# A mixture of experts in pages of 256 tokens: the thirteenth page is cut to 128 rows, and long pages are put ahead of short ones

## The chip, the core and the metric
The kernel runs on one core of a Trainium2 chip. Its metric is the device time of one execution in microseconds. Engines are called PE (TensorE), PEld (its weight loads), DVE (VectorE), ACT (ScalarE), POOL (GpSimd) and SP (SyncE), as the profile has them.

## What is computed
Three layers follow one another. The first is attention with four sink tokens and a window of 128 over 4 batches, 8 heads and 768 positions. The second is a dense layer: `g = h - tanh(h)`, `h = x @ w_in`, then `g @ w_out`. The third, where the change is, sends each of 3072 tokens to one of eight experts:

```python
logits = x @ w_gate + modality_bias[modality_id]
e_idx = np.argmax(logits, axis=1)
gate_w = probs[np.arange(N), e_idx]            # softmax of the logits at e_idx
for e in range(E):
    mask = e_idx == e
    h = np.maximum(x[mask] @ w1[e], 0.0)       # 512 -> 1024
    out[mask] = gate_w[mask, None] * (h @ w2[e])   # 1024 -> 512
```

Counted with the reference on its inputs, two experts get all tokens: 1550 and 1522. In pages of 256 that is seven pages and six. Filled in the order in which tokens come, twelve pages hold 242 tokens or more, and the page opened last, the thirteenth, holds 14.

## The kernel before, in words
Attention and the dense layer run in 12 chunks of 256 tokens. Behind each chunk `r_route` finds the expert of each token, gives each token a slot in a page of 256 slots that belongs to one expert, and writes token number and gate to that slot of a list `xs` in HBM by two scatters on POOL (line 657). `self.rem` holds the free slots of each expert's open page, `self.cur` its next slot, `self.npg` the number of pages so far. Empty slots hold a token number that no write accepts, so that the scatter of the result drops them.

Thirteen pages (`NSTAT`) stand in the main stream, in the order of a table `order` (page and expert of each place). `r_order(False)`, after the eleventh chunk, fills the first three places (`EARLY`) with pages that are already full; `r_order(True)`, after the last, fills the others: rank of each page by a scan (line 684), and then page and expert for each rank by products of 16 x 19 elements and sums over them (lines 692 to 700). SP reads the table into registers (lines 725, 744) and uses them as addresses. What is left, pages from the fourteenth on and the cases that the fast path can't do, stands behind a branch on `self.more` (line 971).

One page is eight blocks of 128 hidden units. `m_list` loads the page's slots of `xs` (line 747), `m_xload` gathers its token rows by two indirect DMAs of 128 rows on POOL (line 762), `m_xT` transposes them on PE (line 773) and splits them into a rounded part and a rest (ACT line 776, DVE line 777). For each block, `m_wload` loads 512 KB of weights, `m_wsplit` splits them on ACT and DVE (lines 738, 739), `m_L1` makes 12 matmuls (line 787; three for each of four 128-slices of the inputs) and the activation (ACT line 790, DVE line 791), `m_L2` makes three matmuls of 512 columns for each of the two halves of 128 tokens (line 804). `m_out` scales the result by the gate (ACT line 812) and scatters 128 rows (POOL line 813), once for each half.

Every operation gets a due time in `m_events` and the like, in units of one block (`t + d` for page start `t` and lead `d`); the events are sorted by it, and a scheduler that simulates the engines then fixes the order in each engine's queue. Each queue is worked in that order. Buffers of one pool go round: the tag `x2` has four, for gathered rows, for results, and for the products of `r_order` (`pv`); sums in PSUM (`macc`) have one buffer for each half. In the table of the order the names `mT2_0`, `macc1_1`, `mx2_0` mean page 2 or 1 and half 0 or 1; `ml2_2` is page 2, block 2.

Of the kernel before, what the change touches and what calls it, by code (L numbers as in the profile page):

```python
# [7 lines left out]
F32 = mybir.dt.float32  # L8
F32R = mybir.dt.float32r
# [31 lines left out]
class Kern:  # L41
# [455 lines left out]
    def r_consts(self):  # L497
# [165 lines left out]
    def r_order(self, last):  # L663
# [7 lines left out]
        bp = lambda ap: ap.unsqueeze(1).to_broadcast([P, NPG, NE])  # L671
        if last:
            v.tensor_scalar(out=sel, in0=self.early, scalar1=-1.0, scalar2=1.0, op0=ALU.mult, op1=ALU.add)
        else:
            end, part, op, big = tl("end", NE), tl("part", NE), tl("op", NPG), cp.tile([P, NPG * NE], F32, tag="pg", name="obig")
            b3 = big.rearrange("p (n e) -> p n e", e=NE)
            v.tensor_add(end, self.cur, self.rem)
            v.tensor_scalar(out=part, in0=self.rem, scalar1=0.0, scalar2=None, op0=ALU.is_gt)
            v.tensor_tensor(out=b3, in0=bn(self.iend), in1=bp(end), op=ALU.is_equal)
            v.tensor_tensor(out=b3, in0=b3, in1=bp(part), op=ALU.mult)  # L680
            v.tensor_reduce(out=op, in_=b3, axis=mybir.AxisListType.X, op=ALU.add)
            v.tensor_scalar(out=sel, in0=self.ipg, scalar1=self.npg, scalar2=None, op0=ALU.is_lt)
            v.tensor_sub(sel, sel, op)
        v.tensor_tensor_scan(out=rk, data0=sel, data1=sel, initial=0.0, op0=ALU.add, op1=ALU.bypass)
# [16 lines left out]
        if last:  # L701
            v.tensor_copy(self.npi, self.npg[:1])

    def r_redo(self, ok):
# [14 lines left out]
        nc.vector.scalar_tensor_tensor(out=t, in0=self.npg, scalar=float(NSTAT), in1=t, op0=ALU.is_le, op1=ALU.mult)  # L719
        self.more = cp.tile([P, 1], I32, name="more")  # L720
# [34 lines left out]
    def m_xload(self, g):  # L755
        nc = self.nc
        pl, idx, src = self.ml[g]
        self.mx[g] = []
        rows = NT - CH if g < EARLY else NT
        for t in range(PG // P):  # L760
# [3 lines left out]
            self.mx[g].append((x, idx[:, t:t + 1], pl[:, t, 0:1]))  # L764

    def m_xT(self, g, t):
        nc = self.nc
        x = self.mx[g][t][0]
        if t == 0:
            self.mxt[g] = self.xtp.tile([P, 2, 4, PG], F32R, tag="xt", name=f"mxt{g}")  # L770
# [8 lines left out]
    def m_L1(self, g, f):  # L779
        nc = self.nc  # L780
        h = self.ps("h", F32, f"mh{g}_{f}")[:, :PG]
# [3 lines left out]
        for k in range(4):  # L785
            for w, xl in ((hi, 0), (hi, 1), (lo, 0)):
                nc.tensor.matmul(h, w[:, k * P:(k + 1) * P], x[:, xl, k], start=(n == 0), stop=(n == 11))  # L787
                n += 1
        gt = self.gp.tile([P, 2, PG], F32R, tag="g", name=f"mg{g}_{f}", bufs=self.o["g"])
# [4 lines left out]
    def m_L2(self, g, f):  # L794
        nc = self.nc
        n8 = FF // P
        if f == 0:
            self.macc[g] = [self.psa.tile([P, DM], F32, tag=f"a{t}", name=f"macc{g}_{t}") for t in range(PG // P)]
# [20 lines left out]
    def m_events(self, add, g, t, t0=-1e9):  # L819
# [9 lines left out]
        at(-x0, self.m_xload, g)  # L829
        for j in range(PG // P):  # L830
            at(-o["mxt"] + 0.5 * j, self.m_xT, g, j)
            at(n8 + o["mlag"] - 0.5, self.m_out, g, j)
        for f in range(n8):
            at(f - o["mwl"], self.m_wload, g, f)
            at(f - o["mws"], self.m_wsplit, g, f)
            at(f, self.m_L1, g, f)
            at(f + o["mlag"], self.m_L2, g, f)
# [198 lines left out]
```

## Time and profile before

| | us |
|---|---|
| median of 3 runs (lowest, highest) | 1171.09 (1169.23, 1175.45) |
| the profiled execution, its own time | 1167.94 |
| its span, first to last instruction | 1166.2 |
| PE busy in the span | 1114.8 |

The page gives shares of the whole span. For a change in one stage it is read by stage: the timeline and the chain of waits from about 1105 us (the last two pages), and from 860 to 885 us (where the last routing, the order and the early pages meet). The profiled execution is 3.15 us below the median.

### The profile page before, as it was taken

What the parts mean: (1) busy time and instruction counts of PE and PEld (TensorE: products, weight loads), DVE (VectorE), ACT (ScalarE), POOL (GpSimd) and SP (SyncE); (2) the same over time, 40 slices, a digit from 0 to 9 for tenths busy, and PEclk for the clock granted to TensorE, in tenths of its full rate; (3) what the DMA queues carried; (4) which work ended last, traced back from release to release, by engine and by line L of the source; (5) the groups of instructions that cost most, each with busy time, mean ns of one, the idle gap of its engine ahead of it and who ended that gap; (6) DMA issues with size and microseconds to landing.
All of it is one profiled execution on the core that took longest, in us unless ns stands there. A gap on an engine that the chain in (4) does not pass through costs nothing.

```text
span 1166.2 us, 22233 instructions
## 1 busy us (share of the span) xinstructions
PE 1114.8 (96%) x7171; PEld 983.8 (84%) x7171; DVE 843.9 (72%) x2229; ACT 697.8 (60%) x1671; POOL 598.1 (51%) x849
## 2 busy tenths in 40 slices
PE   7988889999999999999999999999899999999994
PEld 3456678998999998998999899999788999999994
DVE  3489988787878878797887888756775666666720
ACT  3557556666667666667675766654754556555621
POOL 2367775667676767776676766652322112311210
PEclk9989899999999999999999999999999999999997
DMA  6356322222232222222121312100958776776500
GB/s 200 92 189 227 129 70 49 83 71 73 70 69 81 58 87 68 75 64 87 53 91 55 100 48 87 44 6 28 364 161 251 233 219 210 240 231 220 178 36 4
DMA packets 75117, 137.05 MB, mean 118 GB/s; under 512 B 16240, under 2 KB 51312, under 8 KB 74992
## 3 DMA queue, kind: packets, MB, share of 16 engines
q1 hardware_dynamic: 70064, 122.40, 34.5%
q0 software_dynamic: 4928, 13.14, 3.1%
q8 instruction: 59, 0.97, 0.3%
q14 instruction: 66, 0.54, 0.2%
HBM read 122.86 MB, written 13.17 MB: 117 GB/s over the span
## 4 chain that ended last, share of the span: by engine, by line
PE 76%; DVE 10%; issue 7%; POOL 3%; DMA 1%; ACT 0%; POOLq 0%; DVEq 0%; SPq 0%; ACTq 0%
PE h L176 19%; PE acc L246 18%; PE mh L787 11%; PE macc L804 10%; PE s L315 2%; PE s L312 2%; PE lg L579 2%; PE T L348 2%; PE R L418 2%; PE s L313 1%; DVE K L214 1%; PE T L349 1%; PE R L420 1%; PE R L406 1%; PE xT L572 1%
## 5 line engine op out<-in xcount | busy, mean ns | idle before, releaser
L176 PE MATMUL h<-xt,wi 128*128 128x256 f32 x2304 | 348.3, 289 | 13.3 <-ACT wi L209 5.1
L176 PEld LDWEIGHTS h<-xt,wi 128*128 128x128 f32 x2304 | 311.7, 192 | 32.8 <-ACT wi L209 6.9
L246 PE MATMUL acc<-wo,g 128*128 128x512 f32 x1152 | 315.0, 400 | 4.7 <-ACT g L209 3.7
L246 PEld LDWEIGHTS acc<-wo,g 128*128 128x128 f32 x1152 | 202.5, 190 | 38.4 <-ACT g L209 4.3
L739 DVE TENSOR_TENSOR ml<-mr,mh 128x1024 fp32r<-128x1024 f32 x104 | 128.7, 1242 | 59.7 <-ACT mh L738 57.8
L214 POOL TENSOR_TENSOR g<-gy,g 128x512 fp32r<-128x512 f32 x96 | 130.8, 1362 | 72.5 <-ACT g L209 68.0
L787 PE MATMUL mh<-mxt,mh 128*128 128x256 f32 x832 | 156.1, 283 | 0.7 <-ACT mxt L776 0.7
L804 PE MATMUL macc<-mh,mg 128*128 128x512 f32 x416 | 146.6, 398 | 2.5 <-DVE mg L791 2.5
L787 PEld LDWEIGHTS mh<-mxt,mh 128*128 128x128 f32 x832 | 136.3, 191 | 8.8 <-ACT mxt L776 0.9
L738 ACT CAST mh<-mr 128x1024 fp32r<-128x1024 f32 x104 | 108.9, 1051 | 51.1 <-PE macc L804 31.1
L813 POOL DMA_INDIRECT out_dram<-mo,mi x26 | 27.6, 1061 | 206.5 <-ACT mo L812 202.2
L356 POOL TENSOR_SCALAR_AFFINE_SELECT X<-fl 128x512 fp32r<-128x512 f32 (+1 forms) x192 | 113.2, 612 | 38.7 <-DVE fl L386 23.5
L326 ACT ACTIVATE e<-e,nm 128x160 f32<-128x160 f32 x192 | 81.7, 426 | 80.6 <-DVE nm L324 72.6
L787 PE MATMUL mh<-mxt,ml 128*128 128x256 f32 x416 | 117.6, 284 | 0.0
L191 ACT ACTIVATE u<-u,kt 128x512 f32<-128x512 f32 x96 | 69.4, 723 | 47.0 <-DVE h L190 27.9
L804 PEld LDWEIGHTS macc<-mh,mg 128*128 128x128 f32 x416 | 78.0, 190 | 15.8 <-DVE mg L791 2.9
L214 DVE TENSOR_TENSOR K<-k,K 64x448 fp32r<-64x448 f32 x82 | 85.6, 1044 | 2.7
L214 POOL TENSOR_TENSOR B<-q,A 128x256 fp32r<-128x256 f32 x82 | 70.3, 857 | 33.5 <-ACT A L209 33.3
L324 DVE CUSTOM_DVE_ANT_0 e<-s,mask 128x160 f32<-128x160 f32 x192 | 61.1, 318 | 35.6 <-PE T L349 26.0
L790 ACT ACTIVATE mg<-mh 128x256 fp32r<-128x256 f32 x104 | 40.1, 386 | 73.2 <-PE mh L787 69.8
L804 PE MATMUL macc<-ml,mg 128*128 128x512 f32 x208 | 82.6, 397 | 0.0
L187 ACT ACTIVATE u<-h 128x512 f32<-128x512 f32 x96 | 56.5, 588 | 39.2 <-PE h L176 38.9
(214 smaller groups left out, 2206.4 us busy)
## 6 DMA issues: line engine op xcount, KB each, us to landing
mr<-in_moe_w_dram SPq DMA_DIRECT2D x104, 512.0 KB
k<-in_k_dram SPq DMA_DIRECT2D x82, 224.0 KB
v<-in_v_dram SPq DMA_DIRECT2D x96, 128.0 KB
q<-in_q_dram SPq DMA_DIRECT2D x82, 128.0 KB
rawi<-in_moe_w_in_dram SPq DMA_DIRECT2D x16, 512.0 KB
rawo<-in_moe_w_out_dram SPq DMA_DIRECT2D x16, 512.0 KB
x2d<-x SPq DMA_DIRECT2D x24, 256.0 KB
k<-in_k_dram SPq DMA_DIRECT2D x14, 112.0 KB
```

Of the source, the lines that this page charges most:

```text
L176: nc.tensor.matmul(h, w[:, wl, k * P:(k + 1) * P], x[:, xl, k], start=(n == 0), stop=(n == 11))
L187: nc.scalar.activation(u, h, AF.Square)
L191: nc.scalar.activation(u, u, AF.Relu, bias=self.kt, accum_out=self.over[:, n:n + 1])
L214: (self.nc.vector if eng == "v" else self.nc.gpsimd).tensor_tensor(out=out, in0=a, in1=b, op=ALU.subtract)
L246: nc.tensor.matmul(o, g[:, gl, q:q + P], w[:, wl], start=(f == 0 and n == 0), stop=(f == NF - 1 and n == 2))
L324: nc.vector.tensor_tensor_reduce(out=e, in0=s[:, P:QW], in1=self.mask[min(i, 2)], scale=-0.125, scalar=3.0e38, op0=ALU.add, op1=ALU.min, a ...
L326: nc.scalar.activation(e, e, AF.Exp, bias=nm, scale=-1.0, accum_out=u["sm"][:, t:t + 1])
L356: self.nc.gpsimd.affine_select(out=out, in_=in_, pattern=[[0, n], [s, P]], base=0, channel_multiplier=-s, compare_op=ALU.is_gt if prev els ...
L738: nc.scalar.copy(hi, r)
L739: nc.vector.tensor_sub(lo, r, f32(hi))
L787: nc.tensor.matmul(h, w[:, k * P:(k + 1) * P], x[:, xl, k], start=(n == 0), stop=(n == 11))
L804: nc.tensor.matmul(self.macc[g][t], gt[:, gl, t * P:(t + 1) * P], w[:, DM:], start=(f == 0 and n == 0), stop=(f == n8 - 1 and n == 2))
```

## The change
Of the thirteenth place only the first half (128 rows) stays in the main stream: gather, transposes, matmuls, activation and result take a list of halves `ts`, which is `(0,)` there and `(0, 1)` elsewhere. Its second half moves behind the branch. `r_order(True)` now ranks pages with more than 128 tokens ahead of the others, so that the page at the thirteenth place has more than 128 only if ten such pages stand outside the early three; that is `self.half`, which also makes `self.more` true. So that it can tell, it uses `rem`, `cur` and `npg` as the last chunk leaves them, where the rank before came from `early` alone and only the experts (`pexp`) waited for the last chunk. Line numbers shift: 738, 739, 747, 762, 787, 791, 804 and 813 become 753, 754, 762, 777, 803, 807, 820 and 829; 657 becomes 658; 692 to 700 become 705 to 713.

```diff
--- before.py
+++ after.py
@@ r_consts
+        self.half = cp.tile([P, 1], F32, name="half")
-        self.npi = cp.tile([1, 1], I32, name="npi")
+        self.npi = cp.tile([1, 2], I32, name="npi")
@@ r_order(last)
+        end, part, op, big = tl("end", NE), tl("part", NE), tl("op", NPG), cp.tile([P, NPG * NE], F32, tag="pg", name=nm + "big")
+        b3 = big.rearrange("p (n e) -> p n e", e=NE)
+        v.tensor_add(end, self.cur, self.rem)
+        v.tensor_scalar(out=part, in0=self.rem, scalar1=float(PG // 2) if last else 0.0, scalar2=None,
+                        op0=ALU.is_ge if last else ALU.is_gt)
+        v.tensor_tensor(out=b3, in0=bn(self.iend), in1=bp(end), op=ALU.is_equal)
+        v.tensor_tensor(out=b3, in0=b3, in1=bp(part), op=ALU.mult)
+        v.tensor_reduce(out=op, in_=b3, axis=mybir.AxisListType.X, op=ALU.add)
+        v.tensor_scalar(out=sel, in0=self.ipg, scalar1=self.npg, scalar2=None, op0=ALU.is_lt)
+        v.tensor_sub(sel, sel, op)
         if last:
-            v.tensor_scalar(out=sel, in0=self.early, scalar1=-1.0, scalar2=1.0, op0=ALU.mult, op1=ALU.add)
+            all_, rs = tl("all", NPG), tl("rs", NPG)
+            v.tensor_scalar(out=all_, in0=self.early, scalar1=-1.0, scalar2=1.0, op0=ALU.mult, op1=ALU.add)
+            v.tensor_mul(sel, sel, all_)
+            v.tensor_tensor_scan(out=rk, data0=sel, data1=sel, initial=0.0, op0=ALU.add, op1=ALU.bypass)
+            v.tensor_sub(op, all_, sel)
+            v.tensor_tensor_scan(out=rs, data0=op, data1=op, initial=rk[:, NPG - 1:], op0=ALU.add, op1=ALU.bypass)
+            v.tensor_scalar(out=self.half, in0=rk[:, NPG - 1:], scalar1=float(NSTAT - EARLY), scalar2=None, op0=ALU.is_ge)
+            v.tensor_mul(rk, rk, sel)
+            v.tensor_mul(rs, rs, op)
+            v.tensor_add(rk, rk, rs)
+            sel = all_
         else:
...
+            v.tensor_tensor_scan(out=rk, data0=sel, data1=sel, initial=0.0, op0=ALU.add, op1=ALU.bypass)
         v.tensor_sub(rk, rk, sel)
...
-            v.tensor_copy(self.npi, self.npg[:1])
+            v.tensor_copy(self.npi[:, :1], self.npg[:1])
+            v.tensor_copy(self.npi[:, 1:], self.half[:1])
@@ r_redo
         nc.vector.scalar_tensor_tensor(out=t, in0=self.npg, scalar=float(NSTAT), in1=t, op0=ALU.is_le, op1=ALU.mult)
+        nc.vector.scalar_tensor_tensor(out=t, in0=self.half, scalar=0.0, in1=t, op0=ALU.is_equal, op1=ALU.mult)
@@ m_xload, m_xT, m_L1, m_L2, m_events: a list ts of row blocks
-        for t in range(PG // P):
+        for t in ts:
...
-    def m_L1(self, g, f):
+    def m_L1(self, g, f, ts):
+        c0, w = ts[0] * P, len(ts) * P
-        h = self.ps("h", F32, f"mh{g}_{f}")[:, :PG]
+        h = self.ps("h", F32, f"mh{g}_{f}")[:, :w]
...
-                nc.tensor.matmul(h, w[:, k * P:(k + 1) * P], x[:, xl, k], start=(n == 0), stop=(n == 11))
+                nc.tensor.matmul(h, wt[:, k * P:(k + 1) * P], x[:, xl, k, c0:c0 + w], start=(n == 0), stop=(n == 11))
...
-        for t in range(PG // P):
+        for i, t in enumerate(ts):
...
-                nc.tensor.matmul(self.macc[g][t], gt[:, gl, t * P:(t + 1) * P], w[:, DM:],
+                nc.tensor.matmul(self.macc[g][t], gt[:, gl, i * P:(i + 1) * P], w[:, DM:],
@@ run_chunks
             for g in range(NSTAT):
                 self.m_events(add, g, 16.0 * nch + self.o["mt0"] + FF // P * g,
-                              first if g < EARLY else t2 + self.o["trr"] + .35)
+                              first if g < EARLY else t2 + self.o["trr"] + .35,
+                              (0, 1) if g < NSTAT - 1 else (0,))
@@ more_pages
+            half = nc.values_load(self.npi[0:1, 1:2], min_val=0, max_val=1)
             np_ = nc.values_load(self.npi[0:1, 0:1], min_val=0, max_val=NPG)
+            def page(g, ts=(0, 1)):
+                ev = []
+                self.m_events(lambda t, fn, *a: ev.append((t, len(ev), fn, a)), g, 0.0, ts=ts)
+                self.emit(ev)
+            with tc.If(half == 1):
+                page(NSTAT - 1, (1,))
```

POOL, behind the last routing: the two scatters to `xs` stand behind the gathers of page 2 before:

```order
L762 DMA mx2_0_12228<-x2d_64,ms2_11561 128x512
L762 DMA mx2_1_12230<-x2d_64,ms2_11561 128x512
L657 DMA xs_63<-pl_336,sl11_12141 4864x2 x2
L813 DMA out_0_dram<-mo0_0_12270,mi0_11527 3072x512
L813 DMA out_0_dram<-mo0_1_12275,mi0_11527 3072x512
```

and now:

```order
L658 DMA xs_63<-pl_336,sl11_12142 4864x2 x2
L777 DMA mx2_0_12251<-x2d_64,ms2_11562 128x512
L777 DMA mx2_1_12253<-x2d_64,ms2_11562 128x512
L829 DMA out_0_dram<-mo0_0_12293,mi0_11528 3072x512
L829 DMA out_0_dram<-mo0_1_12298,mi0_11528 3072x512
```

The gathers of page 2 have moved behind the two scatters; the rest keeps its order.

VectorE, from the last slots of the routing on (`sl`). Before, the order was written by then, and the queue went on with weights (`ml`) and activations (`mg`):

```order
L649 CAST sl11_12141<-slf11_12140 128x2
L777 TENSOR_TENSOR mxt1_12177<-mT1_1_12219,mxt1_12177 128x4x128
L721 TENSOR_SCALAR more_12201<-ovt_12195 128x1
L739 TENSOR_TENSOR ml2_2_12464<-mr2_2_12258,mh2_2_12463 128x1024
L791 SCALAR_TENSOR_TENSOR mg1_0_12255<-mh1_0_12242,mg1_0_12255 128x256
L739 TENSOR_TENSOR ml2_3_12518<-mr2_3_12296,mh2_3_12517 128x1024
L791 SCALAR_TENSOR_TENSOR mg1_1_12293<-mh1_1_12280,mg1_1_12293 128x256
L739 TENSOR_TENSOR ml2_4_12546<-mr2_4_12326,mh2_4_12545 128x1024
L751 SCALAR_TENSOR_TENSOR ms3_12505<-mpl3_12501 128x2
L739 TENSOR_TENSOR ml2_5_12586<-mr2_5_12363,mh2_5_12585 128x1024
L791 SCALAR_TENSOR_TENSOR mg1_2_12323<-mh1_2_12310,mg1_2_12323 128x256
```

Now the order's operations stand there. These are the last twelve of them, behind fifteen on rows of 1 to 152 elements that come after `sl`:

```order
L736 TENSOR_SCALAR more_12224<-ovt_12217 128x1
L807 SCALAR_TENSOR_TENSOR mg1_0_12278<-mh1_0_12265,mg1_0_12278 128x256
L694 TENSOR_TENSOR olrk_12163<-olrk_12163,olrs_12176 128x19
L698 TENSOR_TENSOR olrk_12163<-olrk_12163,olall_12175 128x19
L705 TENSOR_TENSOR olpv_12187<-ipg_332,olrk_12163 128x304
L807 SCALAR_TENSOR_TENSOR mg1_1_12316<-mh1_1_12303,mg1_1_12316 128x256
L706 TENSOR_TENSOR olpv_12187<-olpv_12187,olall_12175 128x304
L709 TENSOR_TENSOR olpv_12187<-olpv_12187,ipg_332 128x304
L710 TENSOR_REDUCE olres_12190<-olpv_12187 128x16
L709 TENSOR_TENSOR olpv_12187<-olpv_12187,pexp_342 128x304
L713 CAST order_344<-olres_12190 1x16
L710 TENSOR_REDUCE olres_12190<-olpv_12187 128x16
```

All sixteen-rank products have moved behind the routing, with two activations (`mg1_0`, `mg1_1`) between; the weights `ml2_2` come behind them.

PE, at the first sums of page 1. Before:

```order
L773 MATMUL mT2_1_12483<-ident_69,mx2_1_12230 128x128 x4
L804 MATMUL macc1_0_12298<-mh1_0_12039,mg1_0_12255 128x512
L804 MATMUL macc1_0_12298<-ml1_0_12040,mg1_0_12255 128x512
L804 MATMUL macc1_1_12299<-mh1_0_12039,mg1_0_12255 128x512
L804 MATMUL macc1_1_12299<-ml1_0_12040,mg1_0_12255 128x512
```

and now:

```order
L803 MATMUL mh1_3_12361<-mxt1_12199,ml1_3_12262 128x256
L788 MATMUL mT2_0_12479<-ident_69,mx2_0_12251 128x128 x4
L788 MATMUL mT2_1_12506<-ident_69,mx2_1_12253 128x128 x4
L820 MATMUL macc1_1_12322<-mh1_0_12040,mg1_0_12278 128x512
L820 MATMUL macc1_1_12322<-ml1_0_12041,mg1_0_12278 128x512
```

Both transposes of page 2 have moved behind the fourth block of page 1, and the sums of the second half (`macc1_1`) of blocks 0 and 1 behind those.

## Rows read from the trace of the kernel before

**Rows 1.** The page, part 1: busy time, share of the span and instructions of each engine.
```profile
PE 1114.8 (96%) x7171; PEld 983.8 (84%) x7171; DVE 843.9 (72%) x2229; ACT 697.8 (60%) x1671; POOL 598.1 (51%) x849
```
**Rows 2.** The chain that ended last, from 1060 us: start us, us, what.
```profile
1105.15 0.44 PE mT L773 x4
...
1114.89 1.39 PE macc L804 x6
1116.27 1.43 PE mh L787 x12
```
**Rows 3.** Busy time in the stretch of the thirteenth page: engines, PEclk, DMA share, GB/s.
```profile
1128.30:1151.50 23.20, 23.14 (x147) 20.68 (x145) 3.54 (x9) 4.58 (x11) 1.95 (x2) 1.00 0.06 22
```
**Rows 4.** Timeline of weight loads from 399.8 us: start us, us, what.
```profile
399.89 0.19 PEld L416 LDWEIGHTS R<-X,V 128*128 128x128 f32 x1
400.00 0.30 PEld L418 LDWEIGHTS R<-X,V 128*128 128x128 f32 x2
400.23 0.30 PEld L420 LDWEIGHTS R<-X,V 128*128 128x128 f32 x2
400.45 0.42 PEld L176 LDWEIGHTS h<-xt,wi 128*128 128x128 f32 x3
```
**Rows 5.** The chain, from 835 us: gate logits, eight columns each.
```profile
848.62 0.79 PE lg L579 x8
```
**Rows 6.** POOL at the end, then DMA queues from 1148 us on.
```profile
1152.22 0.97 POOL L813 DMA_INDIRECT out_dram<-mo,mi  x1 [20.16 <-ACT mo L812]
1153.49 0.97 POOL L813 DMA_INDIRECT out_dram<-mo,mi  x1 [0.30 <-issue]
...
q0 software_dynamic: 160, 0.03, 0.9%
```
**Rows 7.** Timeline of VectorE: first order, at 806 us; second order, at 865 us.
```profile
806.78 0.16 DVE L677 TENSOR_TENSOR oeend<-cur,rem 128x8 f32<-128x8 f32 x1
...
806.98 0.32 DVE L679 TENSOR_TENSOR obig<-iend,oeend 128x152 f32<-128x152 f32 x1
807.33 0.32 DVE L680 TENSOR_TENSOR obig<-obig,oepart 128x152 f32<-128x152 f32 x1
...
808.69 0.18 DVE L687 SCALAR_TENSOR_TENSOR early<-oerk,oesel 128x19 f32<-128x19 f32 x1
...
865.10 0.47 DVE L696 TENSOR_TENSOR olpv<-olpv,pexp 128x304 bf16<-128x304 bf16 x1
...
865.70 0.46 DVE L697 TENSOR_REDUCE olres<-olpv 128x16 f32<-128x304 bf16 x1
...
866.60 0.15 DVE L649 CAST sl<-slf 128x2 int32<-128x2 f32 x1
```
**Rows 8.** Matmuls and VectorE at page 1, the chain there, and a window after it.
```profile
866.65 0.51 PE L787 MATMUL mh<-mxt,mh 128*128 128x256 f32 x2 [0.68 <-ACT mxt L776]
...
879.76 0.73 PE L804 MATMUL macc<-mh,mg 128*128 128x512 f32 x2 [2.45 <-DVE mg L791]
...
878.01 0.16 DVE L751 SCALAR_TENSOR_TENSOR ms<-mpl 128x2 int32<-128x2 f32 x1 [3.83 <-DMA mpl<-xs]
...
868.35 6.98 DMA xs<-pl,sl
...
880.00:884.00 4.00, 4.00 (x18) 3.62 (x18) 2.74 (x4) 2.10 (x4) 2.24 (x2) 0.60 0.90 296
```
**Rows 9.** DMA issues of the whole span: median us from issue to landing.
```profile
mx<-x2d,ms POOLq DMA_INDIRECT x26, 6.7
...
xs<-pl,sl POOLq DMA_INDIRECT x24, 3.9
```
**Rows 10.** Timeline of matmuls inside that window.
```profile
881.84 0.63 PE L787 MATMUL mh<-mxt,mh 128*128 128x256 f32 x2
...
882.48 0.63 PE L804 MATMUL macc<-mh,mg 128*128 128x512 f32 x1
882.91 0.63 PE L804 MATMUL macc<-ml,mg 128*128 128x512 f32 x1
```

More of the change, by code (lines that the diff above doesn't have):

```diff
@@ L671, in r_order @@
         bp = lambda ap: ap.unsqueeze(1).to_broadcast([P, NPG, NE])
-        if last:
-            v.tensor_scalar(out=sel, in0=self.early, scalar1=-1.0, scalar2=1.0, op0=ALU.mult, op1=ALU.add)
-        else:
[L675 to L683, printed above, removed]
@@ L785, in m_L1 @@
         for k in range(4):
-            for w, xl in ((hi, 0), (hi, 1), (lo, 0)):
-                nc.tensor.matmul(h, w[:, k * P:(k + 1) * P], x[:, xl, k], start=(n == 0), stop=(n == 11))
+            for wt, xl in ((hi, 0), (hi, 1), (lo, 0)):
+                nc.tensor.matmul(h, wt[:, k * P:(k + 1) * P], x[:, xl, k, c0:c0 + w], start=(n == 0), stop=(n == 11))
                 n += 1
-        gt = self.gp.tile([P, 2, PG], F32R, tag="g", name=f"mg{g}_{f}", bufs=self.o["g"])
+        gt = self.gp.tile([P, 2, PG], F32R, tag="g", name=f"mg{g}_{f}", bufs=self.o["g"])[:, :, :w]
         nc.scalar.activation(gt[:, 0], h, AF.Relu)
@@ L792, in m_L1, with m_L2 @@
         self.mg[g, f] = gt
-    def m_L2(self, g, f):
+    def m_L2(self, g, f, ts):
         nc = self.nc
@@ L797, in m_L2 @@
         if f == 0:
-            self.macc[g] = [self.psa.tile([P, DM], F32, tag=f"a{t}", name=f"macc{g}_{t}") for t in range(PG // P)]
+            self.macc[g] = {t: self.psa.tile([P, DM], F32, tag=f"a{t}", name=f"macc{g}_{t}") for t in ts}
         gt = self.mg.pop((g, f))
         hi, lo = self.mw.pop((g, f))
-        for t in range(PG // P):
+        for i, t in enumerate(ts):
             n = 0
             for gl, w in ((0, hi), (0, lo), (1, hi)):
-                nc.tensor.matmul(self.macc[g][t], gt[:, gl, t * P:(t + 1) * P], w[:, DM:],
+                nc.tensor.matmul(self.macc[g][t], gt[:, gl, i * P:(i + 1) * P], w[:, DM:],
                                  start=(f == 0 and n == 0), stop=(f == n8 - 1 and n == 2))
@@ L817, in m_out, with m_events @@
         self.sc = i.ins
-    def m_events(self, add, g, t, t0=-1e9):
+    def m_events(self, add, g, t, t0=-1e9, ts=(0, 1)):
         n8 = FF // P
@@ L828, in m_events @@
             at(-x0 - .01, self.m_list, g)
-        at(-x0, self.m_xload, g)
-        for j in range(PG // P):
-            at(-o["mxt"] + 0.5 * j, self.m_xT, g, j)
+        at(-x0, self.m_xload, g, ts)
+        for j in ts:
+            at(-o["mxt"] + 0.5 * j, self.m_xT, g, j, ts)
             at(n8 + o["mlag"] - 0.5, self.m_out, g, j)
@@ L835, in m_events @@
             at(f - o["mws"], self.m_wsplit, g, f)
-            at(f, self.m_L1, g, f)
-            at(f + o["mlag"], self.m_L2, g, f)
+            at(f, self.m_L1, g, f, ts)
+            at(f + o["mlag"], self.m_L2, g, f, ts)
     def emit(self, ev):
@@ L944, in rest @@
                 with tc.If(np_ > g):
-                    ev = []
-                    self.m_events(lambda t, fn, *a: ev.append((t, len(ev), fn, a)), g, 0.0)
-                    self.emit(ev)
+                    page(g)
                     rest(g + 1)
```

11 lines of the change are left out of this document (5 added, 6 removed).

## The prediction
> **What bounds the kernel now.** The page comes first: PE is busy for 96% of the span and no other engine over 84% [rows 1], so only what PE does, or waits for, can move the end. The chain that ended last comes second. In the last pages it runs on PE alone, in a fixed pattern: 1.43 us for the 12 matmuls of a block's first layer, 1.39 us for the six of its second, and 0.44 us for each half's four transposes [rows 2]. That is 0.119 us for a matmul of 256 columns and 0.232 us for one of 512. The window of the thirteenth page shows PE busy for 23.14 of 23.20 us at a granted clock of 1.00, with DVE, ACT and POOL nearly idle and DMA at 0.06 [rows 3]: weights are in place, and a cut of PE's work shows at the end. Behind PE stand two scatters on POOL, 1.27 us apart [rows 6]. The third view is the timeline at page 1, where the last routing meets the early pages. PE waited 2.45 us there for an activation, because DVE stood for 3.83 us at the list of page 3, which waited for the scatters to `xs` [rows 8]. The clock then fell: 0.60 in the window from 880 to 884 us [rows 8].
>
> **The half page.** The table gives the thirteenth place to the page with 14 tokens, in both kernels: the scatters at the end moved 0.03 MB, some 15 rows of 2 KB, where one half of full rows is 0.26 MB [rows 6]. Its second half is all padding. Nine pages with over 128 tokens stand outside the early three (twelve less three), less than ten, so `half` is 0 and the branch isn't taken. What goes:
> - Second layer: 24 of 48 matmuls of 512 columns, 24 x 0.232 = **5.57 us**.
> - First layer: the 96 matmuls stay, with 128 columns in place of 256. Their weight loads stay whole, and the trace has their price: loads beside matmuls of 128 columns start 0.11 us apart (399.89, 400.00; the two from 400.23 to 400.45) [rows 4], and transposes of 128 columns take 0.44 / 4 = 0.11 [rows 2]. Even matmuls of eight columns take 0.79 / 8 = 0.099 [rows 5]. So half the columns are nearly as dear: 96 x (0.119 - 0.11) = **0.86 us**. Ends: nothing (0.119 each), and 1.9 us (0.099 each). I take 0.11, from the rows with the same columns.
> - Transposes of the second half: **0.44 us** [rows 2].
> - The last scatter: the end moves up by the distance of the two, **1.27 us** [rows 6]; what follows it is the same.
>
> The Trainium skill, TensorE: Matmul & The Clock Gate, section Back-to-back issue gap, speaks of a stream of weight loads and matmuls that runs at about 81 ns a matmul with 128 columns. By it the first layer would give back 96 x 0.038 = 3.6 us in place of 0.86. The rows above, on this kernel's four-byte weights, show 110 ns, and the measurement decides.
>
> Activations and splits of the half page are shorter, and their engines idle [rows 3]. Its weights still come whole, under page 11. Together this is 8.14 us, all on the path.
>
> **The order, which must now wait for the last chunk.** Before, 16-rank products ran ahead of the routing's end, and only a product, a sum and a cast came late. Now all of it comes behind `sl`, which itself is done some 0.85 us earlier than 866.60, since two long operations ahead of it are gone [rows 7]. The first order did the like of eight of the new operations in 808.69 - 806.78 = 1.9 us, 0.35 apart where they have 152 elements [rows 7]. Seven small ones more are about 1.2 us, six long ones 6 x 0.52 = 3.1 (0.47 and a gap) [rows 7], four small ones 0.6, and the three operations between (a split, two activations) 1.5: 8.3 us, so the table is ready near 874 us, not 866. Who waits:
> - SP, which reads the table for page 3's list and weights. Page 3 starts two pages of over 23 us [rows 3] after page 1, which began at 866.65 [rows 8]. Eight microseconds are covered. If the cover were gone, PE would wait for the rest.
> - ACT: the result of page 0's second half goes to the buffer that holds the products. ACT stops there until the last sum, and activations and splits queue behind it. The order has PE's sums `macc1_1`, which need that result taken out, three blocks' work later.
> - DVE's splits of page 2 come later, but page 2 is a page away.
> - POOL: the gathers of page 2 now issue behind the scatters: those at about 866.1 and 867.4, the gathers at 868.7 and 870.0. With 6.7 us to landing [rows 9] the rows are there at 875.4 and 876.7.
>
> PE from 866.65 on: four blocks of first layer are 5.7 us, three sums each of two blocks 1.4, the wait for the split 0.6: it comes to page 2's transposes at 874.3. There it waits 1.1 us, and 0.85 more for the second half. This stands in the place of the old 2.45 us, for page 3's list now lands when DVE has weights to split. I take a gain of 0.4 us. Ends: both the old wait and the low clock behind it go ((1 - 0.60) x 4.0 = 1.6 us more [rows 8]), with no new wait, a gain of 4.1; or the new wait adds to what DVE does late, a loss of 3.
>
> **Sum.** 8.14 + 0.4 = 8.5 us. The profiled execution took 1167.94, so 1159.4; it lies 3.15 below the median of the runs, so the forecast for a median is **1162.5 us**.
>
> **Rivals.**
> - *More comes back.* The wait at page 1 goes with its low clock (12.2 us in all, 1158.8), or matmuls of 128 columns cost half of those with 256 (96 x 0.06 = 5.7 in place of 0.86, so 13.3 us in all, 1157.7). For: the list is no longer ahead of the weights on DVE; the chain's x4 and x8 groups are too short to be a steady stream [rows 2, 5]. Against: weight loads 0.11 apart [rows 4]. Chance 0.15.
> - *A new wait at the order.* If DVE's late chain takes six microseconds more than worked out, ACT is released near 881 us, `macc1_1` with it, and PE waits some 4 us over the old wait: -8.14 + 4 and up to 1.6 for the clock, 1167 to 1168.6. For: every one of some thirty operations waits for the one before, in one queue with activations that PE needs. Against: prices from the same operations [rows 7], and no other work in the queue. Chance 0.12; it counts as no change.
> - *Slower: PE falls to its lower level in the half page.* With 128 columns the array works for less of the time. At 1.2 GHz three first-layer matmuls took 882.48 - 881.84 = 0.64 us, and one of 512 columns 0.43 [rows 10]; the half page would be 96 x 0.213 + 24 x 0.43 = 30.8 us in place of 16.1, which is 14.6 more and 6 us slower than before: 1177. It decides from the point where 8.5 / 14.6 = 58% of the page runs at that level. For: the level fell soon after a wait of 2.45 us [rows 8]. Against: PE has a next matmul ready all through this page [rows 3], and weight loads go on without a gap. Chance 0.04.
> - *It doesn't do what it says.* If `half` were 1, the second half would run behind the branch with its own weight loads, 16 us of PE's work and more: over 1175. The 0.03 MB [rows 6] speak against it. Chance 0.01.
>
> **Numbers.** The forecast has the other 0.68, with 1159.5 to 1165.5 by the ends of its terms. About 0.5%, 5.9 us, is what a measurement of this kernel can tell from no change. Forecast and first rival are faster, 0.83; the new wait is no change, 0.12; the last two are slower, 0.05. The range, 1157 to 1168, takes in the first rival and most of the second.
>
> **What would show it.** First layer of the thirteenth page: 96 matmuls of 128 columns, 0.11 us apart; 600 second-layer matmuls in place of 624; one scatter at the end. PE's span for that page is 16 to 16.5 us against 23.2. At page 1, PE waits for the transposes of page 2, two microseconds in all, and the table is cast near 874 us. The prediction is wrong if spacing is 0.06 or 0.12, if the clock there is below 1.00, or if PE waits more than 5 us between 866 and 885.

## The result, and the profile after

The changed kernel took 1159.42 us (median of 4 runs, 1158.06 to 1160.81) against 1170.38 for the kernel before in the same session (4 runs, 1169.23 to 1175.45): a ratio of 0.9898, 95% interval 0.9866 to 0.9930, so 11 us less. Two later timings, of six runs each, gave 0.9907 (0.9874 to 0.9941) and 0.9900 (0.9863 to 0.9937). The forecast was 1162.5, in a range of 1157 to 1168. The profiled execution took 1158.06 with a span of 1156.3, 9.9 us under the span before.

The page's part 1, which answers to [rows 1]:

```profile
PE 1109.8 (96%) x7143; PEld 978.2 (85%) x7143; DVE 845.4 (73%) x2244; ACT 696.1 (60%) x1669; POOL 586.4 (51%) x847
```

PE has 28 matmuls less: 24 of the second layer and 4 transposes; 96 of the first layer are only shorter. Its busy time falls by 5.0 us and the span by 9.9: the rest is time in which PE waited, or what stands behind its last matmul.

Where the span went is read from the starts of the stages in the timeline (the first first-layer matmul of a chunk or a page); the three columns on the right are the changed kernel's three profiles.

| stage, us | before | after | again | third |
|---|---|---|---|---|
| first chunk to the second | 99.98 | 98.21 | 98.24 | 105.89 |
| second chunk to the twelfth | 626.42 | 626.67 | 626.90 | 626.84 |
| twelfth chunk to the last gate logits | 74.42 | 75.18 | 75.67 | 74.48 |
| last gate logits to page 1 | 11.89 | 11.90 | 11.90 | 11.89 |
| page 1 to page 2 | 27.38 | 25.32 | 24.46 | 24.43 |
| page 2 to page 3 | 23.43 | 23.43 | 23.43 | 23.43 |
| page 3 to page 4 | 23.42 | 23.84 | 23.42 | 23.42 |
| page 4 to page 11 | 163.99 | 163.99 | 164.00 | 163.99 |
| page 11 to the last sum | 46.57 | 40.25 | 40.24 | 40.25 |
| last sum to the end | 14.75 | 13.54 | 13.72 | 13.86 |

From page 1 on, where the change is, the first profile is 9.2 us shorter than before, the other two 10.3 and 10.2; the rest of the 9.9 us lies ahead of page 1 (1.8 less in the first chunk, 1.0 more in the two stretches behind it). The 0.4 us more from page 3 to page 4 in the first profile stand in neither of the others.

**The half page.** 6.3 us come back by the last sum and 0.9 to 1.2 behind it. (The last stage varies by itself: 14.37 to 15.25 us in the four profiles with two scatters at the end, 13.34 to 14.25 in the ten with one.) The window from its first matmul to its last, with columns as in [rows 3]:

```profile
1124.95:1142.80 17.85, 17.85 (x127) 16.16 (x125) 2.79 (x10) 3.48 (x10) 1.94 (x2) 1.00 0.07 29
```

PE waits for nothing, at a clock of 1.00. One block in PE's timeline (start us, us, what; the rows of short matmuls overlap, some 0.28 us long and 0.11 apart, so the starts are read):

```profile
1133.78 0.33 PE L803 MATMUL mh<-mxt,mh 128*128 128x128 f32 x2
1133.95 0.28 PE L803 MATMUL mh<-mxt,ml 128*128 128x128 f32 x1
1134.07 0.39 PE L803 MATMUL mh<-mxt,mh 128*128 128x128 f32 x2
1134.29 0.28 PE L803 MATMUL mh<-mxt,ml 128*128 128x128 f32 x1
...
1135.07 0.44 PE L820 MATMUL macc<-mh,mg 128*128 128x512 f32 x1
...
1135.82 0.33 PE L803 MATMUL mh<-mxt,mh 128*128 128x128 f32 x2
```

From 1133.95 to 1134.07 is one matmul, from 1134.07 to 1134.29 two: 0.11 us each. The twelve take 1.29 us and the three of the second layer 0.75, where it was 1.43 and 1.39 [rows 2]: 2.04 a block in place of 2.82. Behind the last sum only one scatter is left; it answers to the two of [rows 6]:

```profile
1143.80 0.97 POOL L829 DMA_INDIRECT out_dram<-mo,mi  x1 [12.95 <-ACT mo L828]
```

**The order.** On VectorE the slots of the last chunk (`sl`), the end of the table, and page 3's list:

```profile
865.28 0.17 DVE L650 CAST sl<-slf 128x2 int32<-128x2 f32 x1
...
872.92 0.16 DVE L713 CAST order<-olres 1x16 int32<-1x16 f32 x1
...
882.27 0.17 DVE L764 CAST mi<-mpl 128x2 int32<-128x2 f32 x1
```

The list landed at 881.58 us, and VectorE, which came to it from splitting weights, didn't wait for it. On ScalarE the result of page 0's second half, which waits for the buffer of the products:

```profile
872.92 0.69 ACT L828 ACTIVATE mo<-macc,mpl 128x512 f32<-128x512 f32 x1 [2.33 <-DVE olres L710]
```

On POOL the scatters to `xs` and the gathers of page 2, one after the other:

```profile
865.74 1.03 POOL L658 DMA_INDIRECT xs<-pl,sl  x1 [26.17 <-DVE olpart L677]
867.07 1.00 POOL L658 DMA_INDIRECT xs<-pl,sl  x1 [0.30 <-issue]
868.38 0.98 POOL L777 DMA_INDIRECT mx<-x2d,ms  x1 [0.30 <-issue]
869.67 1.13 POOL L777 DMA_INDIRECT mx<-x2d,ms  x1 [0.31 <-PE mh L803]
```

And PE, its waits in page 1 and the transposes of page 3:

```profile
866.70 0.38 PE L803 MATMUL mh<-mxt,mh 128*128 128x256 f32 x1 [0.22 <-DVE mxt L792]
...
875.00 1.38 PE L788 MATMUL mT<-ident,mx 128*128 128x128 f32 x8 [1.14 <-DMA mx<-x2d,ms]
...
891.41 0.60 PE L788 MATMUL mT<-ident,mx 128*128 128x128 f32 x4
```

The wait of 2.45 us behind page 3's list is gone, with one of 1.14 us for page 2's rows in its place, and the granted clock, which was 0.60 in the window behind the old wait [rows 8], stays at 1.00:

```profile
876.00:878.00 2.00, 2.00 (x12) 1.50 (x11) 0.41 (x1) 0.82 (x2) 0.00 (x0) 1.00 0.86 281
880.00:882.00 2.00, 2.00 (x13) 1.74 (x13) 2.00 (x3) 1.93 (x4) 0.00 (x0) 1.00 1.03 393
```

Page 1 to page 2 is 2.1 us shorter than before, and 2.9 in the two later profiles, where the wait for page 2's rows is 0 and 0.27 us.

### The profile page after: what moved, and what is told of

The parts are those of the page before. It is cut to its first block, busy times and chain, and to the rows that moved or that the text cites. A ratio compares the mean times of both kernels' runs of the same rounds, so it can differ in the third digit from the quotient of the medians.

```text
span 1156.3 us, 22180 instructions
## 1 busy us (share of the span) xinstructions
PE 1109.8 (96%) x7143; PEld 978.2 (85%) x7143; DVE 845.4 (73%) x2244; ACT 696.1 (60%) x1669; POOL 586.4 (51%) x847
## 5 line engine op out<-in xcount | busy, mean ns | idle before, releaser
L803 PE MATMUL mh<-mxt,mh 128*128 128x256 f32 (+1 forms) x832 | 154.4, 282 | 1.0 <-ACT mxt L791 0.7
L820 PE MATMUL macc<-mh,mg 128*128 128x512 f32 x400 | 141.6, 399 | 0.2
L803 PE MATMUL mh<-mxt,ml 128*128 128x256 f32 (+1 forms) x416 | 117.0, 282 | 0.0
L820 PEld LDWEIGHTS macc<-mh,mg 128*128 128x128 f32 x400 | 74.4, 189 | 13.3 <-DVE mg L807 1.0
L806 ACT ACTIVATE mg<-mh 128x256 fp32r<-128x256 f32 (+1 forms) x104 | 39.2, 377 | 75.1 <-PE mh L803 70.6
L803 PEld LDWEIGHTS mh<-mxt,ml 128*128 128x128 f32 x416 | 79.3, 191 | 0.0
```

The lines of the kernel that those rows point to most:

```text
L803: nc.tensor.matmul(h, wt[:, k * P:(k + 1) * P], x[:, xl, k, c0:c0 + w], start=(n == 0), stop=(n == 11))
L820: nc.tensor.matmul(self.macc[g][t], gt[:, gl, i * P:(i + 1) * P], w[:, DM:], start=(f == 0 and n == 0), stop=(f == n8 - 1 and n == 2))
```

## The experiments

Theory: the half page and the order are separate gains, some 7.5 us at the end and some 2 to 3 at page 1, the second because VectorE no longer stands at page 3's list ahead of work that PE needs. Rivals: that wait and the low clock behind it vary by themselves; the long order costs something that the half page hides; short matmuls are priced by columns. Ratios are to the kernel before, timed beside.

**half_old_rank: the half page alone**

```diff
-        end, part, op, big = tl("end", NE), tl("part", NE), tl("op", NPG), cp.tile([P, NPG * NE], F32, tag="pg", name=nm + "big")
...
+        if last:
+            v.tensor_scalar(out=sel, in0=self.early, scalar1=-1.0, scalar2=1.0, op0=ALU.mult, op1=ALU.add)
...
-            with tc.If(half == 1):
-                page(NSTAT - 1, (1,))
```

> The half page alone: the rank is the one of before (from `early` alone), so the scatters, the list of page 3 and all else up to the last page stand in the queues as before. It leaves out the guard: a thirteenth page with over 128 tokens would lose its second half. Theory (the two gains are separate, and the order stage gave its 2.1 us by moving page 3's list out of VectorE's way): the half page gives 7.5 us here too (matmuls of 128 columns 0.112 us apart, 2.04 us a block in place of 2.82, one scatter 1.2 us earlier), while at page 1 the wait of 2.45 us behind page 3's list and the granted clock near 0.6 after it are back: page 1 to page 2 start 27.4 us, span 1166.2 - 7.5 = 1158.7. Rival (the wait at page 1 and the low clock vary from execution to execution, and the changed kernel only drew a better one): page 1 to page 2 near 25.3 or less here as well, span 1156.5. Rival (the half page is worth more when nothing else changes, 128-column matmuls hidden behind loads): block under 1.9 us.

Ratio 0.9909 (0.9883 to 0.9935). From page 11 on it is the changed kernel (40.25 us to the last sum, 13.35 behind it). At page 1 the old wait is back, longer. VectorE's timeline there:

```profile
881.30 0.16 DVE L752 SCALAR_TENSOR_TENSOR ms<-mpl 128x2 int32<-128x2 f32 x1 [5.79 <-DMA mpl<-xs]
```

PE's, where it waits for the activation behind that list:

```profile
883.05 0.73 PE L806 MATMUL macc<-mh,mg 128*128 128x512 f32 x2 [3.35 <-DVE mg L793]
```

The windows from then on, with the granted clock third from the end:

```profile
882.00:884.00 2.00, 0.95 (x5) 0.86 (x6) 1.29 (x4) 1.30 (x2) 1.45 (x2) 0.93 0.81 266
884.00:886.00 2.00, 2.00 (x11) 2.00 (x11) 1.34 (x2) 0.99 (x2) 1.84 (x1) 0.50 0.90 309
```

Page 1 to page 2 took 28.27 us. The theory holds: 7.7 us belong to the half page alone (46.57 + 14.75 less 40.25 + 13.35), and the wait and low clock come with the old order of VectorE's queue.

**rank_full_page: the new order alone**

```diff
-                              (0, 1) if g < NSTAT - 1 else (0,))
+                              (0, 1))
...
-            with tc.If(half == 1):
-                page(NSTAT - 1, (1,))
```

> The new order alone: long pages ranked ahead, all of the order behind the last routing, but the thirteenth page is computed whole, as before. Theory: page 1 to page 2 start 25.3 us as in the changed kernel (a wait of 1.1 us for the gathers of page 2, clock 1.00), so 2.1 us come back there and some 0.4 are lost at page 3's list: span 1164.0 to 1164.5, some 2 us under before. Rival (the longer order costs time, and the gain of the changed kernel is all the half page's): span 1166 or more. Last page as before: 2.82 us a block, two scatters 1.27 us apart.

Ratio 0.9969 (0.9949 to 0.9989): the new order by itself is faster. Page 1 to page 2 took 24.56 us, 0.7 less than expected, for the wait for page 2's rows was 0.4 us and not 1.1. PE's waits in that stretch are 0.7 and 0.2 us for page 1's splits and this one (what waited, for what, us in total, times, longest):

```profile
PE mT L788 <- DMA mx<-x2d,ms: 0.4, 1, 0.4
```

The last page is as before (23.15 us, 14.43 behind). The span came out at 1166.6 and not 1164, since the first chunk took 1.3 us more than in the profile of the kernel before (101.2 us) and the stretch from the twelfth chunk to the last logits 1.8 more. The first chunk has nothing of the change and took 96.2 to 105.9 us in the fourteen profiles, which is why only stages and medians are compared here.

**before_late_list and before_pool_list: the kernel before, page 3's list later in VectorE's queue, or on GpSimd**

The first makes the list of page 3, and with it the gathers of its rows, due four blocks later; the second has a page's list (from page 3 on) made into addresses by GpSimd:

```diff
         x0 = o["mxe"] if g == 1 else o["mxl"]
+        x0 -= 4 if g == 3 else 0
```
```diff
-        nc.vector.tensor_copy(idx, pl[:, :, 1])
...
-        nc.vector.scalar_tensor_tensor(out=src, in0=pl[:, :, 1], scalar=float(NT), in1=pl[:, :, 1], op0=ALU.is_lt, op1=ALU.mult)
+        if g >= EARLY:
...
+            nc.gpsimd.tensor_copy(idx, pl[:, :, 1])
+            nc.gpsimd.tensor_scalar(out=lt, in0=pl[:, :, 1], scalar1=float(NT), scalar2=None, op0=ALU.is_lt)
+            nc.gpsimd.tensor_mul(lt, lt, pl[:, :, 1])
+            nc.gpsimd.tensor_copy(src, lt)
...
```

> The kernel before with one edit: the list of page 3 is due four blocks later, so that on VectorE its operation stands behind the split of the last block of page 2's weights. Theory (the old wait came from the place of that operation in VectorE's queue, ahead of weights and activations that PE needs): the wait of 2.45 us and the low clock after it both go, page 1 to page 2 start 23.5 to 24 us in place of 27.4, span 1162.3 to 1162.8. Rival (the low clock comes from something else in this stretch, the load of 0.9 of DMA for one): the wait goes and the clock still falls, page 1 to page 2 near 25, span 1163.8. Rival (the wait only moves to the next thing that is late): 27 us, span 1166.

> The kernel before with the same move of the list's operations to GpSimd and nothing else: PE's and ScalarE's order is that of before, VectorE's differs by those operations alone. Theory (the wait of 2.45 us and the low clock behind it came from VectorE's stand at the list, and from nothing else): page 1 to page 2 start 23.4 us in place of 27.4, no low clock in that stretch, 4.0 us less from page 1 on and all else as before; so of the changed kernel's gain the part at page 1 (2.1 us there) is to be had, and more of it, without a new order. Rival (GpSimd, which stands at the list now, issues the results and rows behind it late): PE waits elsewhere in pages 1 to 3, and less than 2 us come back.

Ratios 0.9960 (0.9937 to 0.9984) and 0.9963 (0.9938 to 0.9988); page 1 to page 2 took 23.39 and 23.15 us, the pace of the other pages. In the first, VectorE stands at the list as long as before, but behind six splits of weights in page 1 and not three:

```profile
881.27 0.17 DVE L749 CAST mi<-mpl 128x2 int32<-128x2 f32 x1 [3.90 <-DMA mpl<-xs]
```

PE waits for nothing behind it. In the second, GpSimd's waits from 866 to 920 us hold the list now:

```profile
POOL mlt L753 <- DMA mpl<-xs: 10.4, 2, 7.8
```

and all that is left of PE's, from 862 to 916 us, is

```profile
PE mh L794 <- ACT mxt L783: 0.7, 1, 0.7
```

So the cause was the place of the list's operations in VectorE's queue, ahead of work that PE needed, and not the stand of 3.8 or 3.9 us as such; 4.0 and 4.2 us were to be had there without any new order.

**own_buffer: the products of the order in a buffer of their own**

```diff
-        pv = self.x2p.tile([P, DM], F32, tag="x2", name=nm + "pv").bitcast(BF16)
-        pick, val = pv[:, :n * NPG], pv[:, DM:DM + n * NPG]
+        pick = cp.tile([P, (NPG - EARLY) * NPG], BF16, tag="opk", name=nm + "pk")[:, :n * NPG]
+        val = cp.tile([P, NPG * NE], F32, tag="pg", name=nm + "pv").bitcast(BF16)[:, :n * NPG]
```

> The changed kernel with one edit: the products of the order lie in a buffer of 608 bytes of their own and in the routing's scratch, no longer in one of the four buffers for rows. The gathers of page 2 then stand ahead of the scatters again, their transposes at page 1's first block, and ScalarE takes out page 0's second half without waiting for the order. Theory (the products' buffer was what put the gathers behind the scatters and held ScalarE 2.33 us): the wait of 1.14 us for the gathers goes, page 1 to page 2 start 23.5 to 24.2 us, span 1154.9 to 1155.5, clock 1.00. Rival (the scatters, now 2.6 us later, make page 3's list late and VectorE waits for it): a wait for the list of some us on VectorE comes back, PE waits over 1 us at page 1 again, span 1156.5 or more.

Ratio 0.9906 (0.9877 to 0.9934), no more than the changed kernel. The wait for page 2's rows is gone and ScalarE takes out page 0 at 863.92 and 865.07 us, but VectorE's timeline has the wait for the list again:

```profile
881.36 0.17 DVE L764 CAST mi<-mpl 128x2 int32<-128x2 f32 x1 [2.34 <-DMA mpl<-xs]
```

and PE's one for ScalarE at the end of the page:

```profile
888.37 0.50 PE L820 MATMUL macc<-mh,mg 128*128 128x512 f32 x1 [0.57 <-ACT mg L806]
```

Page 1 to page 4 took 71.47 us (before 74.23; the changed kernel 72.59, 71.31, 71.28), and that without four of page 2's transposes, 0.44 us, which here (and in the two runs that follow) stand ahead of page 1. The buffer did what was said of it, and what was next in line took the gain.

**own_buffer_late_list and own_buffer_pool_list: both cures together**

Own_buffer with the one or the other of the two edits to the list above.

> Both cures on the changed kernel: the order's products in a buffer of their own, and the list of page 3 due four blocks later. Theory: VectorE no longer waits 2.34 us for that list in page 1, so the 0.57 us that PE waited at its end and the 0.44 us in page 2 go too: page 1 to page 2 start 23.4 to 23.6 us, page 2 to page 3 23.4 us, 1.2 us under own_buffer and 1.9 under the changed kernel from page 1 on; span 1153.5 if the first chunk is as there. Rival (the list, four blocks later, makes the rows of page 3 late): a wait for transposes in page 2, and no gain over own_buffer.

> The changed kernel with the order's products in a buffer of their own, as in own_buffer, and the two operations on the list of a page (its token numbers made integers, from page 3 on) on GpSimd as four small ones, ahead of the gathers that use them; nobody else reads them. SyncE issues the list where it did in own_buffer. Theory (what was left in own_buffer is VectorE's stand of 2.34 us at the list, with weights and activations behind it, and moving the list's due time moved its issue and the stand with it): VectorE waits for no list any more, page 1 to page 2 start 23.3 to 23.6 us, page 2 to page 3 23.43, 1.0 to 1.2 us under own_buffer from page 1 on. Rival (the wait comes back as late rows, since GpSimd stands at the list too): PE waits for transposes of page 3 in page 2.

Both miss. Ratios 0.9925 (0.9900 to 0.9950) and 0.9932 (0.9906 to 0.9958); page 1 to page 2 is 23.10 and 23.12 us, and page 2 to page 3 then 25.64 and 27.64. In the first, SyncE issues the list at 885.47 us, ten later than in own_buffer, and the stand in VectorE's timeline moves with it:

```profile
890.89 0.17 DVE L764 CAST mi<-mpl 128x2 int32<-128x2 f32 x1 [2.17 <-DMA mpl<-xs]
```

PE waits behind it, in page 2:

```profile
894.59 0.73 PE L820 MATMUL macc<-mh,mg 128*128 128x512 f32 x2 [1.91 <-DVE mg L807]
```

In the second, the list is issued as in own_buffer (875.07 us), lands at 880.89, GpSimd's gathers start at 884.08 and 885.44, the rows land at 890.44 and 892.03, and PE has stood at their transposes since 888.06, as its timeline shows:

```profile
890.58 0.63 PE L795 MATMUL mT<-ident,mx 128*128 128x128 f32 x4 [2.52 <-DMA mx<-x2d,ms]
```

Of those 2.52 us, 1.7 come from GpSimd. Two of its four operations on the list stand in its timeline as

```profile
881.63 1.05 POOL L769 TENSOR_TENSOR mlt<-mlt,mpl 128x2 f32<-128x2 f32 x1
882.74 1.06 POOL L770 CAST ms<-mlt 128x2 int32<-128x2 f32 x1
```

where the same two took 0.20 and 0.18 us in before_pool_list; here VectorE was splitting weights at the time (`ml`, 881.40 to 883.76 us).

The windows behind PE's wait:

```profile
890.00:892.00 2.00, 1.42 (x8) 1.31 (x9) 0.00 (x0) 0.52 (x1) 0.00 (x0) 0.83 0.84 338
892.00:894.00 2.00, 2.00 (x11) 2.00 (x10) 0.00 (x0) 0.74 (x2) 1.25 (x2) 0.50 0.08 23
```

PE's queue has the transposes of page 3 at the start of page 2, not of page 3. In the changed kernel's first profile page 3's first rows landed at 890.11 us and were transposed at 891.41: the long order had 1.3 us to spare there. In its other two profiles it was 0.35 and 0.34 us (landed 890.96, transposed 891.31; 897.30, 897.64), against 10.6 with the old order in half_old_rank.

**long_order: 6 us more on the chain**

```diff
+            for _ in range(6 if last else 0):
+                v.tensor_reduce(out=res[:, i * n:(i + 1) * n], in_=v3, axis=mybir.AxisListType.X, op=ALU.add)
```

> The changed kernel with twelve more sums over 304 elements in the order (the two sums of the products are each taken seven times), 6 us more on VectorE's chain: the condition of the rival with the new wait. Theory (ScalarE stands at page 0's second result until the last sum, and PE's sums of page 1's second half wait for ScalarE): the table is cast near 879 us in place of 873, ScalarE goes on then, PE waits 3.5 to 4.5 us more than the 1.4 of the changed kernel at page 1, the granted clock falls behind that wait, and page 1 to page 2 start is 29 to 31 us: 4 to 5.5 us slower. Rival (there is slack in the chain): under 27 us. Rival (6 us cost 6 us and more, since weights queue behind): over 31.5 us.

Ratio 0.9977 (0.9954 to 1.0001). The size is right and the place wrong: page 1 to page 2 took 25.13 us, page 2 to page 3 28.55. On VectorE the table is written at

```profile
885.04 0.17 DVE L715 CAST order<-olres 1x16 int32<-1x16 f32 x1
```

which is 15.8 us after page 1's start, where the changed kernel has 7.0: nine more, not six, since activations of page 1 stand inside the chain now. ScalarE's hold cost PE 0.67 and 0.34 us. The rest came by way of the list (table, list, rows), in page 2 of PE's timeline:

```profile
895.69 0.73 PE L822 MATMUL macc<-mh,mg 128*128 128x512 f32 x2 [1.06 <-DVE mg L809]
901.72 0.63 PE L790 MATMUL mT<-ident,mx 128*128 128x128 f32 x4 [2.09 <-DMA mx<-x2d,ms]
```

with the clock behind it, in the windows:

```profile
902.00:904.00 2.00, 2.00 (x10) 1.62 (x8) 0.62 (x1) 0.34 (x1) 0.00 (x0) 0.68 1.00 401
904.00:906.00 2.00, 2.00 (x11) 1.90 (x10) 1.22 (x1) 0.70 (x1) 0.00 (x0) 0.50 1.03 402
```

**half_64: what a short matmul costs**

```diff
-        c0, w = ts[0] * P, len(ts) * P
+        c0, w = ts[0] * P, len(ts) * P if ts != (0,) else P // 2
...
```

> The changed kernel with the first layer of the thirteenth page cut to 64 columns, and its sums, result and scatter to 64 rows; rows 64 to 127 of that page are left out (here it has 14 tokens). Theory (weight loads set the price of short matmuls): first-layer matmuls stay 0.10 to 0.112 us apart, second-layer matmuls 0.232, a block 1.9 to 2.05 us; the page gives 0 to 1.1 us more. Rival (columns set the price): 0.06 us apart, 1.4 us a block, 5 us more.

Ratio 0.9925 (0.9895 to 0.9956). A block takes 1.97 us in place of 2.04, the page 0.40 less. One block's first layer in PE's timeline:

```profile
1132.19 0.30 PE L803 MATMUL mh<-mxt,mh 128*128 128x64 f32 x2
1132.33 0.28 PE L803 MATMUL mh<-mxt,ml 128*128 128x64 f32 x1
1132.44 0.39 PE L803 MATMUL mh<-mxt,mh 128*128 128x64 f32 x2
1132.67 0.28 PE L803 MATMUL mh<-mxt,ml 128*128 128x64 f32 x1
...
1133.45 0.43 PE L820 MATMUL macc<-mh,mg 128*64 128x512 f32 x1
```

Half the columns again, and the spacing stays 0.11 us. The loads of 128 x 128 weights stand 0.11 us apart too, here beside the block of the changed kernel shown above:

```profile
1133.89 0.19 PEld L803 LDWEIGHTS mh<-mxt,ml 128*128 128x128 f32 x1
1134.01 0.30 PEld L803 LDWEIGHTS mh<-mxt,mh 128*128 128x128 f32 x2
1134.23 0.19 PEld L803 LDWEIGHTS mh<-mxt,ml 128*128 128x128 f32 x1
```

It is no fixed price of a matmul: the two at the head of a block, the first of which has its load beside the last long matmul, start closer together (0.17 us for the two at 128 columns and 0.14 at 64, where later pairs take 0.22 and 0.23). So the load sets the spacing. The Trainium skill, TensorE: Matmul & The Clock Gate, section LDWEIGHTS (loading the stationary operand), puts a load's time in ns at its number of columns divided by 1.2, which for 128 makes an estimate of 107 ns; the trace agrees within some 5 ns (0.111 to 0.112 us).

**after_again and after_third: the changed kernel itself**

> The changed kernel itself once more, to see what of its 9.9 us in the first pair of profiles belongs to it. Theory: from page 1 on it is the same to some tenths (page 1 to page 2 start 24.6 to 25.4 us with a wait of 0.4 to 1.2 us for the gathers, 40.2 us from page 11's start to the last sum), and what differs lies in the first chunk, which took 96.2 to 102.5 us in the six profiles so far whatever the kernel. Rival (the stretch from the last chunk to the last logits, 75.2 to 76.3 us in the three kernels with the new order and 74.4 to 74.7 in the three with the old one, is a cost of the order): over 75 us here too; by the theory it may come out at 74.5.

> The changed kernel a third time, beside the whole kernel of this call. Theory: from page 1 on as in its two profiles so far: page 1 to page 4 start 71.3 to 72.6 us, 53.8 us from page 11's start to the end, ratio near 0.990 to 0.991. Rival (the margin of 1.3 us between the landing of page 3's rows and their transposes is used up in some executions): page 2 to page 3 start over 24 us, with a wait for page 3's rows.

Their stages stand in the table. Page 1 to page 2 is 24.46 and 24.43 us; in the first of them page 2's rows were there in time:

```profile
874.91 1.36 PE L788 MATMUL mT<-ident,mx 128*128 128x128 f32 x8
```

The stretch to the last logits was 75.67 in after_again, as its rival had it, but it is no cost of the order: it is 74.48 in after_third and 74.32 in own_buffer_late_list, and 76.81 in before_pool_list with the old order.

**guard_only: a whole kernel from the parts**

```diff
...
+            v.tensor_mul(lg, lg, sel)
+            v.scalar_tensor_tensor(out=lg, in0=rk, scalar=float(NSTAT - EARLY - 1), in1=lg, op0=ALU.is_equal, op1=ALU.mult)
+            v.tensor_reduce(out=self.half, in_=lg, axis=mybir.AxisListType.X, op=ALU.add)
...
```

(`lg` marks pages with over 128 tokens, found as in the change; `rk` is the rank of before.)

> A whole kernel put together from what the runs showed: the half page; the old rank (from `early` alone, so that the table's products stay ahead of the last routing); a guard that only asks, off the path, whether the page at the thirteenth place has over 128 tokens; and the operations on the lists on GpSimd. It computes the same result for every input, but sends the second half behind the branch more often, since long pages are not put ahead. Theory (half page and list are separate gains, and the new rank was not needed for either on this input): page 1 to page 4 start 70.0 us as in before_pool_list (the changed kernel: 72.6 and 71.3), 53.8 us from page 11's start to the end; so some 11.5 us under before and 1.3 to 2.6 under the changed kernel if the first chunk takes the same, a ratio near 0.990. Rival (the guard's eleven operations on VectorE and the scatters, now ahead of page 2's gathers, make rows of page 2 late): PE waits for transposes at page 1, page 1 to page 4 start over 71 us.

Ratio 0.9918 (0.9890 to 0.9947). By stages it is the best of the kernels that leave nothing out: page 1 to page 4 in 70.26 us, 1.0 to 2.3 under the changed kernel, with nothing left of PE's waits there but the 0.7 for page 1's split, and 53.93 from page 11 to the end. In the timing the two can't be told apart (0.9900 for the changed kernel in the same session). No version tried was measurably faster than the changed kernel.

## Why the prediction was right, point by point

- **What bounds the kernel** held: PE's path sets every stage from page 1 on, and all that came back came from its work, its waits or the tail.
- **Half page, 8.14 us.** Measured 7.5 in the changed kernel's first profile, 7.4 and 7.2 in the other two, 7.7 alone. Second layer and first layer were to give 6.43 by 24 x 0.232 and 96 x 0.009; the middle blocks gave 0.78 each, 6.24 for eight: 0.64 where the three matmuls of 512 were put at 0.70, since the first of the three takes 0.28 us behind short matmuls, and 0.14 where the first layer was put at 0.11. By the last sum it was 6.32 against 6.87 with the transposes. The scatter gave 0.9 to 1.2 in place of 1.27. The estimate of 3.6 us that the prediction works out from the Trainium skill, TensorE: Matmul & The Clock Gate, section Back-to-back issue gap, did not come: the first layer gave 1.1, at 0.111 us a matmul.
- **Page span of 16 to 16.5 us** holds for the page's own matmuls and not for the window: page 12 begins while page 11's sums run, six of them (1.5 us) stand in the window of 17.85, and 16.4 is left. 1.03 us came back ahead of it.
- **The order's chain.** Forecast and measured: `sl` 865.75 and 865.28, table near 874 and 872.92, scatters 866.1 and 867.4 against 865.74 and 867.07, gathers 868.7 and 870.0 against 868.38 and 869.67, PE at page 2's transposes at 874.3 against 873.86, where it waited 1.14 of the 1.1 given. Page 1 began 0.68 us earlier than before (865.97), by what lies ahead of it; counted from its start, each of these lies within 0.4 us of the forecast, and the table came after 6.95 us in place of 7.35. That the wait agrees to 0.04 us is luck: the other two profiles have 0 and 0.27. ScalarE was held until the last sum, as said.
- **The order's gain, 0.4 us**, was the term that was mis-sized: 1.6 to 3.0 (page 1 to page 4). (By its own figures, 2.45 less 1.1 less 0.85, it was 0.5.) Of the 0.85 us for page 2's second half only 0.26 were paid (875.00 to 876.13 us for eight transposes, where two halves take 0.88), since its rows landed 0.66 us behind the first half's while PE had those to transpose; and the low clock did not follow the shorter wait, which the prediction had at 1.6 us, kept out of its sum and in its range (before, page 1 had taken 1.5 us more than 23.43 and its wait). Where the wait itself was 0 or 0.27 us, the gain came to 2.9 and 3.0.
- **"Eight microseconds are covered"** held, but not for its reason: the step looked at page 3's start, but its transposes stand at page 2's start, and only 0.3 to 1.3 us were to spare. long_order and own_buffer_pool_list show what comes when they are gone.
- **The rivals.** *More comes back* came true for the wait and its clock in part, not for short matmuls: by stages 9.2 to 10.3 us came back, between the forecast's 8.5 and this rival's 12.2. *A new wait at the order* has its place in the list's way more than at ScalarE's buffer (there 0.67 and 0.34 us in long_order, 0.66 in half_64); long_order's 6 us of added work cost 4.5 to 5.8 us from page 1 to page 4 (77.11, against 72.59 to 71.28). *Slower by the clock* fell: 1.00 through the half page. *Doesn't do what it says* fell: one scatter, no branch.
- **The forecast lies 3.1 us above the median**: 0.6 to 1.7 of that are what the order gave over its term (1.2 to 2.6), less what the half page fell short (0.6 to 0.9); that the two offset each other is luck. The rest is no more than the medians vary (those of the kernel before lay between 1168.1 and 1170.6 in five sessions). The prediction's 1159.5 to 1165.5 "by the ends of its terms" is narrower than those ends: 4.1 gained or 3 lost at page 1 and 0 to 1.9 for the first layer make 1157.8 to 1166.8.

## What to carry to other kernels

Cutting columns off a matmul saves little once the weight load sets the spacing (here 0.119 us at 256 columns, 0.11 at 128 and at 64); whole matmuls taken away, and whole transfers at the end, are what count. Where an engine that works its queue in order converts data that a transfer brings, look for what is queued behind it: moving two tiny operations off VectorE was worth 4.2 us, and moving them behind the work that PE needed 4.0. Work out the cover of a late value from the first instruction in any queue that uses it, not from the stage it belongs to, and expect the next in line to take part of any wait that goes.

## What the runs showed of the hardware that was not expected

- A wait on PE of 2.45 us [rows 8], 2.52, 3.35, or 1.06 and 2.09 close together, was followed by granted clocks down to 0.50, and its page took 1.5 to 2.0 us more than 23.43 and the wait together; behind waits of 0.57, 1.14 and 1.91 the windows show 1.00.
- A list of 2 KB took 5.7 us to land while the weights' transfers had a DMA share near 1.0 (875.92 to 881.58 us in the changed kernel), against 1.9 from 893.57, at a share of 0.44.
- A GpSimd operation on 128 x 2 elements took 0.18 to 0.23 us by itself or beside an activation on VectorE, and 0.68 to 1.06 where VectorE was splitting weights (1024 elements a partition): in before_pool_list, guard_only and own_buffer_pool_list each of these 51 slow ones ends 0.04 to 0.08 us behind the end of such a split. That is how they fall together in three traces; no run tries it apart.
- The first chunk took 96.2 to 105.9 us in fourteen profiles, the same program included (98.2 and 105.9). PE waits there for weights being converted (4.3 us in total behind ScalarE and 2.4 behind GpSimd in the changed kernel's first profile), and the granted clock differs (0.80 before and 1.00 after, from 54 to 80 us); what makes it long or short was not tried.
